# Where the q, k and v loads of a block are issued, in a sliding-window attention kernel with a highway layer

## The chip, the cores and the metric

The kernel runs on one core of a Trainium2 chip. The metric is the device time of one execution in microseconds. The core has TensorE (matmul, written PE in the profile, with PEld for its weight loads), VectorE (DVE), ScalarE (ACT), GpSimd (POOL) and SyncE (SP), each with an instruction queue of its own that is worked off in order; they are coupled by semaphores. Transfers run on the core's 16 DMA engines. Here GpSimd issues almost all loads, and SyncE issues the stores.

## What is computed

Attention over 4 batches, 8 heads, 768 positions of width 64, with a causal window of 128 positions and 4 sink positions at the start of each sequence; its output, 3072 tokens of 512 numbers, goes through a highway layer:

```
scores = scale * np.matmul(q, k.transpose(0, 1, 3, 2))
keep = (pos[None, :] < n_sink) | ((rel >= 0) & (rel < window))     # rel = pos[:, None] - pos[None, :]
a = exp(where(keep, scores, -1e9) - max);  a = a / (a.sum() + 1e-9)
x = np.matmul(a, v)                                                # as 3072 x 512
H = np.maximum(x @ w_h, 0.0)
T = 1.0 / (1.0 + np.exp(-(x @ w_t + b_t)))
out = T * H + (1.0 - T) * x
```

## The kernel before

The 3072 tokens are 24 blocks of 128. Each block goes through the same steps, and the steps of several blocks overlap. The order is written out by hand: `ORDER` (lines 676 to 704) is a list of entries such as `S:12`, step and block, and a loop (line 709) calls the function that `STEP` (line 652) has for each. Inside the schedule each engine works off its own instructions in exactly this order; semaphores are set where one engine needs another's result. So an entry that is moved past another matters only if both put instructions on the same engine.

The steps, with n the block:

- `S` (`pe_S`, TensorE): transposes of the q and k of a later block (`pe_T`, L323; which one, `hosted` says: from block 8 on, q and k of block n+2; before that q of n+1 and k of n+2), then the scores (L376, and L389 for the edges), all into one PSUM tile from block 9 on.
- `xx` (ScalarE, L403; in early blocks two halves `x0_`, `x1_`, L398): exp of the scores. `tt` (ScalarE, L335; in early blocks `tq`, `tk`, L328): the copy of the transposes to SBUF. `mm` (VectorE, L409; early `m0_`, `m1_`): the mask, in place.
- `A` (`do_A`): `pe_A` on TensorE, the product with v: the edge part `pe_AB` (L434, with v of blocks n-1 and n+1), the block's own v (L453) and the sinks (L459). From block 9 on it begins with `pe_bias` (L442) for the highway gate of block n-1. After `pe_A`, `do_A` issues loads on GpSimd.
- `xh` (VectorE, L467 and L472): reciprocal and normalisation. `X` (TensorE, L486) transposes it, `xT` (ScalarE) or `xTV` (VectorE) copies it out (L491).
- `Mt` and `Mh` (TensorE, L502 and L514): the two 512x512 products of the highway layer. `u` (ScalarE, L507): tanh of the gate. `d` (VectorE, L520): max(H, 0) - x. `U` (VectorE, L526): u + 1. `e` (L531): its product with d. `o` (L536): twice x plus that; then the store, on SyncE's queue.
- `sk`, `es`: scores and exp of the sinks. When k of a new sequence's first block has been transposed, GpSimd fills the sink keys (`fill_ks`, L347, two copies) and the sink values (`sink_v`, L186).

Loads: `load_q`, `load_k`, `load_v` (L112, L119, L126) read fp32 from HBM and write fp16 to SBUF; a k or v block that spans two sequences takes two transfers. The blocks up to 8 have buffers of their own and are loaded at the start, in a fixed order (lines 194 to 238). From block 9 on q and k have three buffers each (`late_pool`), so the load of block m waits until block m-3 has been transposed, and v has five (`v_ring`). q of block 9 is not transposed in an `S`, but in a step of its own, `Tq:9`, which stands between `S:7` and `S:8`. A load waits at the head of GpSimd's queue, and whatever GpSimd has to do after it waits behind it.

Before the change all three loads of a step are issued in `do_A`, in the order v of block n+4, q of block n+6, k of block n+6.

At the start VectorE prepares masks and constants. Two of them concern the change: `ones_row` and `ones2`, with which TensorE adds the gate's bias (`bt16`, two copies of the bias on rows 0 and 64). `ones_row` has row 0 at one and takes one 128-row product; `ones2` is a copy of it with row 64 at one besides, for two products of 64 rows.

Of the kernel before, what the change touches and what calls it, by code (L numbers as in the profile page):

```python
# [8 lines left out]
FP16 = mybir.dt.float16  # L9
# [11 lines left out]
def kernel(  # L21
# [18 lines left out]
    nc = tc.nc  # L40
    P = 128

    B, H, S, D = q.shape
# [10 lines left out]
    NB = NT // P  # L54
# [4 lines left out]
    AHEAD = 8  # L59

    const = ctx.enter_context(tc.tile_pool(name="const", bufs=1))
# [25 lines left out]

    ctx.callback(close_s)
    HP = P // 2
    B0 = 9  # L90
    M0 = 9
    FIRST = 9
    NV = FIRST + 5
# [6 lines left out]
    def vi(n):  # L100
        return n if n < FIRST else FIRST + (n - FIRST) % (NV - FIRST)

    def chunk_parts(n):
        b, c = divmod(n, NSC)
        if c:
            return [(slice(0, P), b, c * P - HP)]
        return ([(slice(0, HP), b - 1, S - HP)] if b else []) + ([(slice(HP, P), b, 0)] if b < B else [])

    def load_q(n):
        b, c = divmod(n, NSC)  # L110
        qsd = (sd_pool if n < FIRST else late_pool).tile([P, H, D], FP16, tag="qsd", name="qsd")
        nc.gpsimd.dma_start(out=qsd, in_=q[b, :, c * P:(c + 1) * P, :].transpose([1, 0, 2]))  # L112
        q_sd[n] = qsd

    def load_k(n):
        ksd = (sd_pool if n < FIRST else late_pool).tile([P, H, D], FP16, tag="ksd", name="ksd")
        for rows, b, s0 in chunk_parts(n):
            nr = rows.stop - rows.start
            nc.gpsimd.dma_start(out=ksd[rows], in_=k[b, :, s0:s0 + nr, :].transpose([1, 0, 2]))  # L119
        k_sd[n] = ksd  # L120
# [20 lines left out]
    bt32 = const.tile([P, DM], FP32, tag="bt32")  # L141
    bt16 = const.tile([P, DM], FP16, tag="bt16")
    ones_row = const.tile([P, P], FP16, tag="ones_row")
    ones2 = const.tile([P, P], FP16, tag="ones2")
    kf_first = const.tile([P, H, D], FP32, tag="kf0", name="kf0")
    ident32 = const.tile([P, P], FP32, tag="ident32")
    ident2 = const.tile([P, P], FP16, tag="ident2")
    ks_bd = [const.tile([P, KW], FP16, tag=f"ks{i}", name=f"ks{i}") for i in range(2)]
    vs_bd = [const.tile([P, H, 65], FP16, tag=f"vs{i}", name=f"vs{i}") for i in range(2)]
# [43 lines left out]
    with tc.manual_schedule(engines={ENG.Pool, ENG.SP}):  # L193
# [7 lines left out]
        for b in range(B):  # L201
            nc.sync.dma_start(out=vs_dn[b], in_=v[b, :, 0:NSINK, :])
        nc.gpsimd.affine_select(
            out=ident, in_=ident, compare_op=ALU.is_equal, fill=0.0,
# [57 lines left out]
    def bias_rows(_):  # L262
        nc.vector.memset(bt16, 0.0)
        nc.vector.memset(ones_row, 0.0)
        nc.vector.memset(ones_row[0:1, :], 1.0)
        nc.vector.tensor_copy(out=ones2, in_=ones_row)
        nc.vector.memset(ones2[HP:HP + 1, :], 1.0)

    def bias_half(_):
        for r in (0, HP):  # L270
# [13 lines left out]
    def m_tile():  # L284
        return m_bank[int(next(m_next))]
# [7 lines left out]
    av_t, xh_of, xT_of, t_of, u_of, h_of, dd_of, ee_of, sk_of = {}, {}, {}, {}, {}, {}, {}, {}, {}  # L293
# [127 lines left out]
    def av_tile(n):  # L421
        if n not in av_of:
            av_of[n] = av_ps.tile([P, 2, 4, P], FP32, tag="av", name="av")
            av_t[n] = av_of[n]
        return av_of[n]

    def pe_AB(n):
        av = av_tile(n)
        nxt = v_ring[vi(n + 1)]
        prv = v_ring[vi(n - 1 if n % NSC else n)]  # L430
        lo, hi = slice(0, HP), slice(HP, P)
        for j in range(H):
            for src, part, vt, h in ((lo, hi, nxt, j), (hi, lo, prv, (j + 4) % H)):
                nc.tensor.matmul(  # L434
                    av[part, h // 4, h % 4, 0:_AVN], lhsT=e_at(n, h)[src, P:EW],
                    rhs=vt[src, 65 * h:65 * h + _AVN], start=(h % 4 == 0), stop=False,
                    skip_group_check=True)

    def pe_bias(n):
        t_of[n] = m_tile()  # L440
        for rows in (slice(0, HP), slice(HP, P)):
            nc.tensor.matmul(t_of[n][rows, :], lhsT=ones2[rows, rows], rhs=bt16[rows, :],  # L442
                             start=True, stop=False, skip_group_check=True)

    def pe_A(n):
        if n >= B0:
            pe_bias(n - 1)
        pe_AB(n)
        av = av_of[n]
        vt = v_ring[vi(n)]  # L450
        b, c = divmod(n, NSC)
        for h in range(H):
            nc.tensor.matmul(  # L453
                av[:, h // 4, h % 4, 0:_AVN], lhsT=e_at(n, h)[:, 0:P],
                rhs=vt[:, 65 * h:65 * h + _AVN], start=False,
                stop=False, skip_group_check=True)
        if c:
            for g in range(2):
                nc.tensor.matmul(  # L459
                    av[:, g, :, 0:65], lhsT=es_of[n],  # L460
                    rhs=vs_bd[b % 2][:, 4 * g:4 * g + 4, :], start=False, stop=True,
                    skip_group_check=True)
        av_of[n] = av.rearrange("p g h e -> p (g h) e")
# [167 lines left out]
    def new_T(m, g):  # L631
        if g and m and m % NSC == 0 and m < NB:
            fill_ks(m // NSC, nc.gpsimd)
            sink_v(m // NSC, nc.gpsimd)

    def do_A(n):
        pe_A(n)
        if FIRST <= n + 4 <= NB:
            load_v(n + 4)
        if AHEAD <= n + 6 < NB:  # L640
            load_q(n + 6)
        if FIRST <= n + 6 <= NB:
            load_k(n + 6)

    def norm(n):
        dve_rec(n)
# [2 lines left out]
    def spare(t):  # L649
# [5 lines left out]
        "tqV": lambda n: copy_T(n, 0, nc.vector.tensor_copy),  # L655
        "tkV": lambda n: copy_T(n, 1, nc.vector.tensor_copy),
        "xx": act_SS, "tt": both_T, "mm": dve_masks,
        "S": pe_S, "x0_": lambda n: act_S(n, 0), "x1_": lambda n: act_S(n, 1),
        "m0_": lambda n: dve_mask(n, 0), "m1_": lambda n: dve_mask(n, 1),
        "sk": pe_sink, "es": act_sink, "A": do_A, "xh": norm,  # L660
        "X": pe_X, "xT": act_X, "xTV": lambda n: act_X(n, nc.vector.tensor_copy),
        "Mh": pe_Mh, "Mt": pe_Mt, "u": act_u, "U": dve_U, "d": dve_d, "e": dve_e, "o": dve_o,
        "mz0_": first_mask, "mz1_": second_mask, "id": identities, "ma": clear_ks,
        "na": clear_vs, "mc": bias_rows, "fa": lambda _: fill_ks(0, nc.vector), "fb": bias_half,
        "fc": sink_ones, "fd": lambda _: sink_v(0, nc.vector), "cv": convert_v,
# [9 lines left out]
    }  # L675
    ORDER = """
    mz0_:0 ma:0 na:0 Tq:0 na:1 Tk:0 tq:0 mz1_:0 tk:0 ma:1 wA:0 wA:0 Tk:1 mc:0 cv:0 tk:1 fa:0
    wA:0 wA:0 wA:0 S:0 cv:1 x0_:0 fb:0 x1_:0 wA:0 wA:0 wA:0 wA:0 Tq:3 m0_:0 fc:0 tq:3 wA:0 Tk:2
    tk:2 m1_:0 fd:0 wA:0 wA:0 wA:0 wA:0 Tq:1 A:0 tq:1 S:1 xh:0 sk:1 x0_:1 x1_:1 Tq:2 m0_:1 X:0
    sk:3 xTV:0 es:1 Tk:3 m1_:1 tq:2 tk:3 wA:1 A:1 es:3 S:2 xh:1 x0_:2 x1_:2 Tk:4 m0_:2 sk:2  # L680
    tkV:4 X:1 es:2 m1_:2 S:3 xT:1 A:2 x0_:3 Mh:1 x1_:3 xh:2 tq:4 d:1 X:2 tk:5 Mh:0 xTV:2 m0_:3
    Mh:2 d:0 m1_:3 S:4 d:2 Mt:0 x0_:4 x1_:4 m0_:4 A:3 u:0 m1_:4 Mt:1 tq:5 xh:3 tk:6 U:0 sk:4 u:1
    e:0 S:5 es:4 o:0 X:3 x0_:5 U:1 sk:5 xTV:3 e:1 A:4 x1_:5 m0_:5 o:1 tq:6 Mt:2 xh:4 tk:7 es:5
    u:2 m1_:5 X:4 S:6 xT:4 U:2 e:2 A:5 x0_:6 o:2 Mh:3 x1_:6 xh:5 tq:7 Mh:4 m0_:6 tk:8 m1_:6 X:5
    d:3 S:7 xT:5 d:4 A:6 x0_:7 Mh:5 xh:6 x1_:7 Mt:3 d:5 tq:8 tk:9 m0_:7 X:6 u:3 m1_:7 Mt:5 xT:6
    U:3 e:3 sk:7 o:3 u:5 Tq:9 es:7 U:5 Mt:4 tq:9 e:5 o:5 S:8 u:4 U:4 A:7 x0_:8 e:4 o:4 Mt:6
# [2 lines left out]
    mm:10 u:8 X:9 d:8 S:11 xT:9 U:8 A:10 e:8 xx:11 o:8 sk:11 xh:10 Mt:9 es:11 tt:11 mm:11 Mh:9  # L689
    u:9 X:10 d:9 S:12 xT:10 U:9 A:11 e:9 xx:12 o:9 Mt:10 xh:11 tt:12 Mh:10 mm:12 u:10 X:11 d:10  # L690
    S:13 xT:11 U:10 A:12 e:10 xx:13 o:10 sk:13 xh:12 Mt:11 es:13 tt:13 mm:13 Mh:11 u:11 X:12
    d:11 S:14 xT:12 U:11 A:13 e:11 xx:14 o:11 Mh:12 xh:13 tt:14 Mt:12 mm:14 X:13 d:12 u:12 S:15
    xT:13 U:12 e:12 xx:15 A:14 o:12 sk:15 xh:14 Mt:13 tt:15 mm:15 es:15 X:14 S:16 u:13 xTV:14
    U:13 A:15 xx:16 Mh:14 xh:15 tt:16 Mt:14 d:14 mm:16 Mh:13 u:14 U:14 sk:17 d:13 X:15 es:17
    S:17 xT:15 e:13 e:14 A:16 xx:17 o:13 o:14 Mt:15 xh:16 tt:17 Mh:15 mm:17 u:15 X:16 S:18 d:15
    xT:16 U:15 A:17 xx:18 e:15 o:15 Mh:16 xh:17 tt:18 Mt:16 mm:18 X:17 u:16 S:19 xTV:17 d:16
    A:18 xx:19 U:16 e:16 sk:19 xh:18 Mt:17 es:19 mm:19 tt:19 Mh:17 o:16 u:17 X:18 S:20 d:17
    xT:18 U:17 A:19 xx:20 e:17 o:17 Mh:18 xh:19 tt:20 Mt:18 mm:20 X:19 u:18 S:21 xTV:19 d:18
    A:20 xx:21 U:18 e:18 sk:21 o:18 Mt:19 es:21 xh:20 tt:21 Mh:19 mm:21 u:19 X:20 S:22 d:19
    xT:20 U:19 A:21 xx:22 e:19 o:19 Mh:20 xh:21 tk:24 Mt:20 mm:22 X:21 u:20 S:23 xTV:21 d:20  # L700
    A:22 xx:23 U:20 e:20 sk:23 xh:22 Mt:21 es:23 mm:23 X:22 u:21 Mh:21 xT:22 o:20 A:23 d:21 U:21
# [45 lines left out]
```

## Time and profile before

| what | value |
|---|---|
| median of 3 runs (lowest, highest) | 120.45 us (120.37, 120.69) |
| the profiled execution's own time | 134.59 us |
| its span, first to last instruction | 132.5 us |
| mean granted TensorE clock in it | 0.76 |
| GpSimd, q loads: issues, mean time of one | 23, 908 ns |
| GpSimd, k loads | 26, 856 ns |
| GpSimd, v loads | 26, 853 ns |
| q loads, median from issue to landing | 5.7 us |
| GpSimd waiting for edge matmuls before a v load | 14.0 us, 7 times |
| GpSimd waiting for transposes before a q load | 11.9 us, 2 times |

The profile is one execution, and it took 14 us longer than the runs did. Busy times of an engine are sums of its instructions' durations. [...] A row of the timeline reads: start in us from the span's start, duration in us, engine, line, operation, what it writes and reads, and in brackets how long the engine was idle before it and what ended that.

### The profile page before, as it was taken

The numbers are of one execution on the slowest core, as the hardware profiler recorded it, in microseconds if no ns is written. First come the engines' busy times: TensorE is split into PE (matmuls) and PEld (weight loads), VectorE is DVE, ScalarE is ACT, GpSimd is POOL, SyncE is SP. The second block draws the span as 40 slices with busy tenths as digits, with TensorE's granted clock in tenths as the row PEclk, the third lists the DMA queues.
The fourth block names the chain that finished last, engine by engine and source line by source line (L and its number), as shares of the span: only waits on it lengthen the run. The fifth ranks groups of instructions, "written<-read, shape, count | busy, mean of one in ns | idle before, by whom it ended". The sixth has DMA issues, their size and how long they took to land.

```text
span 132.5 us, 4975 instructions
## 1 busy us (share of the span) xinstructions
PE 122.8 (93%) x2119; PEld 69.7 (53%) x2119; DVE 106.5 (80%) x254; ACT 88.0 (66%) x123; POOL 72.2 (55%) x97
## 2 busy tenths in 40 slices
PE   5998879997999999999999999999999999999940
PEld 2444556444555464754666556647655664565520
DVE  6889745959897769968978797689979978977980
ACT  3356679196696668848977888768769868673120
POOL 6999878589940069926749466596591400000000
PEclk9977777777777777777777777777777777777775
DMA  3999999999999039999599999999999392202122
GB/s 90 217 158 147 161 181 195 155 138 123 185 194 153 2 90 190 190 196 137 56 178 158 153 161 140 171 97 96 180 187 131 103 127 84 79 5 79 54 105 79
DMA packets 79848, 17.64 MB, mean 133 GB/s; under 512 B 75602, under 2 KB 76882, under 8 KB 79828
## 3 DMA queue, kind: packets, MB, share of 16 engines
q0 software_dynamic: 71888, 9.97, 121.7%
q1 hardware_dynamic: 6884, 7.12, 17.7%
q10 hardware_dynamic: 1056, 0.26, 1.2%
q8 instruction: 16, 0.26, 0.8%
q14 instruction: 4, 0.03, 0.1%
HBM read 21.01 MB, written 6.29 MB: 206 GB/s over the span
## 4 chain that ended last, share of the span: by engine, by line
PE 81%; DVE 12%; ACT 2%; issue 2%; DVEq 0%
PE m L514 20%; PE m L502 19%; PE av L453 7%; PE av L434 6%; PE sps L323 5%; PE sps L376 4%; PE av L459 4%; PE sps L389 4%; PE m L358 4%; PE av L486 4%; PE m L499 2%; ACT e L398 1%; DVE u L526 1%; PE m L442 1%; DVE v L178 1%
## 5 line engine op out<-in xcount | busy, mean ns | idle before, releaser
L126 POOL DMA_DIRECT2D v<-in_v_dram x26 | 22.1, 853 | 18.4 <-PE av L434 14.0
L502 PE MATMUL m<-wt_sb,xT 128*128 128x512 f16 x92 | 30.4, 463 | 0.0
L514 PE MATMUL m<-wh_sb,xT 128*128 128x512 f16 x92 | 29.5, 458 | 0.0
L112 POOL DMA_DIRECT2D qsd<-in_q_dram x23 | 20.8, 908 | 11.9 <-PE sps L323 11.9
L403 ACT ACTIVATE e<-sps,ebias 128x1536 f16<-128x1536 f32 x15 | 23.1, 1541 | 4.4 <-PE sps L389 4.3
L409 DVE TENSOR_TENSOR e<-e,mask 128x768 f16<-128x768 f16 (+1 forms) x33 | 23.9, 732 | 2.5 <-ACT e L398 2.5
L507 ACT ACTIVATE u<-m 128x512 f16<-128x512 f32 x23 | 13.8, 598 | 13.7 <-PE m L502 13.7
L119 POOL DMA_DIRECT2D ksd<-in_k_dram x26 | 22.1, 856 | 0.5 <-DMA ksd<-in_k_dram 0.3
L398 ACT ACTIVATE e<-sps,ebias 128x768 f16<-128x768 f32 x18 | 15.2, 897 | 6.7 <-PE sps L389 6.5
L520 DVE SCALAR_TENSOR_TENSOR dd<-m,xh 128x512 f16<-128x512 f32 x23 | 15.8, 688 | 4.6 <-PE m L514 4.4
L472 DVE TENSOR_TENSOR xh<-av,rec 128x512 f16<-128x512 f32 x24 | 16.6, 691 | 0.8
L514 PEld LDWEIGHTS <-xT 128*128 128x128 f16 x92 | 10.0, 112 | 12.1 <-issue 10.8
L536 DVE SCALAR_TENSOR_TENSOR otok<-xh,ee 128x512 f32<-128x512 f16 x23 | 15.8, 689 | 0.6
L502 PEld LDWEIGHTS <-xT 128*128 128x128 f16 x92 | 9.9, 110 | 11.4 <-issue 10.8
L335 ACT COPY tt<-sps 128x1024 f16<-128x1024 f16 x13 | 13.0, 997 | 0.0
L434 PE MATMUL av<-v,e 64*64 64x66 f16 x384 | 11.2, 196 | 1.3 <-DVE xT L491 1.1
L491 ACT COPY xT<-av 128x512 f16<-128x512 f16 x15 | 8.7, 581 | 4.9 <-PE av L486 4.9
L526 DVE TENSOR_SCALAR u<-u 128x512 f16<-128x512 f16 x23 | 9.2, 400 | 2.9 <-ACT u L507 2.8
L434 PEld LDWEIGHTS <-e 64*64 64x64 f16 x384 | 9.5, 109 | 2.9 <-issue 2.3
L328 ACT COPY t<-sps 128x512 f16<-128x512 f16 x19 | 10.3, 589 | 1.1 <-PE sps L323 1.1
L453 PE MATMUL av<-v,e 128*128 128x66 f16 x192 | 10.7, 198 | 0.0
L486 PEld LDWEIGHTS <-xh 64*128 64x128 f16 x192 | 4.2, 95 | 11.6 <-DVE e L409 7.9
(94 smaller groups left out, 183.3 us busy)
## 6 DMA issues: line engine op xcount, KB each, us to landing
out_dram<-otok SPq DMA_DIRECT2D x23, 256.0 KB, 3.2
qsd<-in_q_dram POOLq DMA_DIRECT2D x23, 128.0 KB, 5.7
ksd<-in_k_dram POOLq DMA_DIRECT2D x19, 128.0 KB, 5.7
v<-in_v_dram POOLq DMA_DIRECT2D x19, 128.0 KB, 5.4
wh_sb<-in_moe_w_h_dram POOLq DMA_DIRECT2D x1, 512.0 KB, 7.5
wt_sb<-in_moe_w_t_dram POOLq DMA_DIRECT2D x1, 512.0 KB, 8.9
ksd<-in_k_dram POOLq DMA_DIRECT2D x7, 64.0 KB, 5.2
v<-in_v_dram POOLq DMA_DIRECT2D x7, 64.0 KB, 5.5
```

Of the source, the lines that this page charges most:

```text
L112: nc.gpsimd.dma_start(out=qsd, in_=q[b, :, c * P:(c + 1) * P, :].transpose([1, 0, 2]))
L119: nc.gpsimd.dma_start(out=ksd[rows], in_=k[b, :, s0:s0 + nr, :].transpose([1, 0, 2]))
L126: nc.gpsimd.dma_start(out=vt[rows, :, 0:D], in_=v[b, :, s0:s0 + nr, :].transpose([1, 0, 2]))
L398: nc.scalar.activation(out=e_tile(n)[:, g].rearrange("p a b c -> p a (b c)"), in_=s_tile(n, g)[:, :, 0:2 * EW], func=AF.Exp, bias=ebias, s ...
L403: nc.scalar.activation(out=e_tile(n).rearrange("p g a b c -> p (g a) (b c)"), in_=s_of[n][:, :, 0:2 * EW], func=AF.Exp, bias=ebias, scale= ...
L409: nc.vector.tensor_tensor(out=ev, in0=ev, in1=m.unsqueeze(1).to_broadcast([P, k, EW]), op=ALU.mult)
L434: nc.tensor.matmul(av[part, h // 4, h % 4, 0:_AVN], lhsT=e_at(n, h)[src, P:EW], rhs=vt[src, 65 * h:65 * h + _AVN], start=(h % 4 == 0), sto ...
L453: nc.tensor.matmul(av[:, h // 4, h % 4, 0:_AVN], lhsT=e_at(n, h)[:, 0:P], rhs=vt[:, 65 * h:65 * h + _AVN], start=False, stop=False, skip_g ...
L472: nc.vector.tensor_tensor(out=xh.rearrange("p (h d) -> p h d", d=D), in0=av_of.pop(n)[:, :, 0:D], in1=rec_of.pop(n).unsqueeze(2).to_broadc ...
L502: nc.tensor.matmul(t_of[n], lhsT=xT[:, kc, :], rhs=wt_sb[:, kc, :], start=False, stop=(kc == NOC - 1), skip_group_check=True)
L514: nc.tensor.matmul(hps, lhsT=xT[:, kc, :], rhs=wh_sb[:, kc, :], start=(kc == 0), stop=(kc == NOC - 1))
L520: nc.vector.scalar_tensor_tensor(out=dd, in0=h_of.pop(n), scalar=0.0, in1=xh_of[n], op0=ALU.max, op1=ALU.subtract)
```

## The change

Three things are changed. First, the loads: q of block n+5 is issued behind `S:n`, v of block n+4 behind `A:n` as before, and k behind `d`, where the blocks are counted through in order (each `d`, in the order in which they stand, takes the next k, the first one block 7; those below 9 are loaded at the start and left out). Ahead of a k load GpSimd copies one element of that `d`'s result into a tile `turn`. Second, `ones2` goes: `ones_row` now has row 0 at one in its first 64 columns and row 64 at one in its last 64, and serves both kinds of product. Third, the bias products move from `pe_bias` into `pe_AB`, at the same place; the table `T_BESIDE` names the same blocks as `B0` did, and with `LATE` at 99 the second branch is not taken. In `ORDER` some neighbours are exchanged; of these only one exchange concerns two steps on the same engine, `cv:1` and `fb:0` on VectorE at the start: the bias is now scaled (L271) before the v of block 1 is converted (L178).

```
-        nc.vector.memset(ones_row[0:1, :], 1.0)
-        nc.vector.tensor_copy(out=ones2, in_=ones_row)
-        nc.vector.memset(ones2[HP:HP + 1, :], 1.0)
+        nc.vector.memset(ones_row[0:1, 0:HP], 1.0)
+        nc.vector.memset(ones_row[HP:HP + 1, HP:P], 1.0)
...
+        m = T_BESIDE.get(n)
+        if m is not None:
+            t_of[m] = m_tile()
+            if n < LATE:
+                for part in (lo, hi):
+                    nc.tensor.matmul(
+                        t_of[m][part, :], lhsT=ones_row[part, part], rhs=bt16[part, :],
+                        start=True, stop=False, skip_group_check=True)
...
+    def do_S(n):
+        pe_S(n)
+        if AHEAD <= n + 5 < NB:
+            load_q(n + 5)
+
+    k_next = iter(range(AHEAD - 1, NB + 1))
+
+    def do_d(n):
+        dve_d(n)
+        m = next(k_next, None)
+        if m is not None and m >= FIRST:
+            nc.gpsimd.tensor_copy(out=turn, in_=dd_of[n][0:1, 0:1])
+            load_k(m)
+
     def do_A(n):
         pe_A(n)
         if FIRST <= n + 4 <= NB:
             load_v(n + 4)
-        if AHEAD <= n + 6 < NB:
-            load_q(n + 6)
-        if FIRST <= n + 6 <= NB:
-            load_k(n + 6)
...
-    wA:0 wA:0 wA:0 S:0 cv:1 x0_:0 fb:0 x1_:0
+    wA:0 wA:0 wA:0 S:0 fb:0 x0_:0 cv:1 x1_:0
```

More of the change, by code (lines that the diff above doesn't have):

```diff
@@ L89 @@
     HP = P // 2
-    B0 = 9
+    T_BESIDE = {9: 8, 10: 9, 11: 10, 12: 11, 13: 12, 14: 13, 15: 14, 16: 15, 17: 16, 18: 17, 19: 18, 20: 19, 21: 20, 22: 21, 23: 22}
+    LATE = 99
     M0 = 9
@@ L143 @@
     ones_row = const.tile([P, P], FP16, tag="ones_row")
-    ones2 = const.tile([P, P], FP16, tag="ones2")
     kf_first = const.tile([P, H, D], FP32, tag="kf0", name="kf0")
     ident32 = const.tile([P, P], FP32, tag="ident32")
+    turn = const.tile([1, 1], FP16, tag="turn")
     ident2 = const.tile([P, P], FP16, tag="ident2")
@@ L437, in pe_AB @@
                     skip_group_check=True)
[L439 to L443, printed above, removed]
+            if m is not None and n >= LATE and j % 2 == 0:
+                cols = slice(D * j, D * j + 2 * D)
+                for part in (lo, hi):
+                    nc.tensor.matmul(
+                        t_of[m][part, cols], lhsT=ones_row[part, part], rhs=bt16[part, cols],
+                        start=(j == 0), stop=False, skip_group_check=True)
     def pe_A(n):
-        if n >= B0:
-            pe_bias(n - 1)
         pe_AB(n)
@@ L657 @@
         "xx": act_SS, "tt": both_T, "mm": dve_masks,
-        "S": pe_S, "x0_": lambda n: act_S(n, 0), "x1_": lambda n: act_S(n, 1),
+        "S": do_S, "x0_": lambda n: act_S(n, 0), "x1_": lambda n: act_S(n, 1),
         "m0_": lambda n: dve_mask(n, 0), "m1_": lambda n: dve_mask(n, 1),
@@ L661 @@
         "X": pe_X, "xT": act_X, "xTV": lambda n: act_X(n, nc.vector.tensor_copy),
-        "Mh": pe_Mh, "Mt": pe_Mt, "u": act_u, "U": dve_U, "d": dve_d, "e": dve_e, "o": dve_o,
+        "Mh": pe_Mh, "Mt": pe_Mt, "u": act_u, "U": dve_U, "d": do_d, "e": dve_e, "o": dve_o,
         "mz0_": first_mask, "mz1_": second_mask, "id": identities, "ma": clear_ks,
@@ L677 @@
     mz0_:0 ma:0 na:0 Tq:0 na:1 Tk:0 tq:0 mz1_:0 tk:0 ma:1 wA:0 wA:0 Tk:1 mc:0 cv:0 tk:1 fa:0
-    wA:0 wA:0 wA:0 S:0 cv:1 x0_:0 fb:0 x1_:0 wA:0 wA:0 wA:0 wA:0 Tq:3 m0_:0 fc:0 tq:3 wA:0 Tk:2
+    wA:0 wA:0 wA:0 S:0 fb:0 x0_:0 cv:1 x1_:0 wA:0 wA:0 wA:0 wA:0 Tq:3 m0_:0 fc:0 tq:3 wA:0 Tk:2
     tk:2 m1_:0 fd:0 wA:0 wA:0 wA:0 wA:0 Tq:1 A:0 tq:1 S:1 xh:0 sk:1 x0_:1 x1_:1 Tq:2 m0_:1 X:0
@@ L682 @@
     Mh:2 d:0 m1_:3 S:4 d:2 Mt:0 x0_:4 x1_:4 m0_:4 A:3 u:0 m1_:4 Mt:1 tq:5 xh:3 tk:6 U:0 sk:4 u:1
-    e:0 S:5 es:4 o:0 X:3 x0_:5 U:1 sk:5 xTV:3 e:1 A:4 x1_:5 m0_:5 o:1 tq:6 Mt:2 xh:4 tk:7 es:5
+    e:0 S:5 es:4 o:0 X:3 x0_:5 U:1 sk:5 xTV:3 e:1 A:4 x1_:5 m0_:5 o:1 tq:6 Mt:2 tk:7 xh:4 es:5
     u:2 m1_:5 X:4 S:6 xT:4 U:2 e:2 A:5 x0_:6 o:2 Mh:3 x1_:6 xh:5 tq:7 Mh:4 m0_:6 tk:8 m1_:6 X:5
@@ L691 @@
     S:13 xT:11 U:10 A:12 e:10 xx:13 o:10 sk:13 xh:12 Mt:11 es:13 tt:13 mm:13 Mh:11 u:11 X:12
-    d:11 S:14 xT:12 U:11 A:13 e:11 xx:14 o:11 Mh:12 xh:13 tt:14 Mt:12 mm:14 X:13 d:12 u:12 S:15
+    d:11 S:14 xT:12 U:11 A:13 e:11 xx:14 o:11 Mh:12 xh:13 tt:14 Mt:12 mm:14 X:13 u:12 d:12 S:15
     xT:13 U:12 e:12 xx:15 A:14 o:12 sk:15 xh:14 Mt:13 tt:15 mm:15 es:15 X:14 S:16 u:13 xTV:14
@@ L696 @@
     xT:16 U:15 A:17 xx:18 e:15 o:15 Mh:16 xh:17 tt:18 Mt:16 mm:18 X:17 u:16 S:19 xTV:17 d:16
[L697 to L701, printed above, removed]
+    A:18 xx:19 U:16 e:16 sk:19 xh:18 Mt:17 es:19 mm:19 tt:19 Mh:17 o:16 u:17 X:18 S:20 xT:18
+    d:17 U:17 A:19 xx:20 e:17 o:17 Mh:18 xh:19 tt:20 Mt:18 mm:20 X:19 u:18 S:21 xTV:19 d:18 A:20
+    xx:21 U:18 e:18 sk:21 o:18 Mt:19 es:21 xh:20 tt:21 Mh:19 mm:21 u:19 X:20 S:22 d:19 xT:20
+    U:19 A:21 xx:22 e:19 o:19 Mh:20 xh:21 tk:24 Mt:20 mm:22 X:21 u:20 S:23 xTV:21 d:20 A:22
+    xx:23 U:20 e:20 sk:23 Mt:21 xh:22 es:23 mm:23 X:22 u:21 Mh:21 xT:22 o:20 A:23 d:21 U:21
     Mt:22 xh:23 e:21 X:23 u:22 Mh:22 xTV:23 o:21 Ta:23 d:22 Ha:23 ua:23 U:22 e:22 Tb:23 da:23
```

## The prediction

> **What bounds the kernel now.** I read the page from the top, then the waits, then timelines of VectorE, GpSimd and TensorE for the stretches that the change touches.
>
> ```profile
> span 132.5 us, 4975 instructions
> ...
> PE 122.8 (93%) x2119; PEld 69.7 (53%) x2119; DVE 106.5 (80%) x254; ACT 88.0 (66%) x123; POOL 72.2 (55%) x97
> ...
> PEclk9977777777777777777777777777777777777775
> ...
> PE 81%; DVE 12%; ACT 2%; issue 2%; DVEq 0%
> ```
>
> The profiled execution took 134.59 us: its span of 132.5 and 2.1 around it. In it TensorE ran at a granted clock of 0.75 after the first 7 us and was busy without a gap from 40 to 125 us, so it bounds that execution, and the chain says so. The median of the runs shown is 120.45 us, 14.1 less, a span of about 118.4. Nothing in the code explains that but the clock: 122.8 us at 0.76 is 93 us at full clock, while VectorE's 106.5 us doesn't scale and is 90% of 118.4. So in the timed runs I take VectorE as the bound from about 40 us on, with latency chains before that, and I price each step in microseconds of VectorE or of a chain. At the profile's clock the same steps cost less, since TensorE covers them (55 to 99 us: PE 44.00 of 44, DVE 36.67).
>
> VectorE's `u + 1` (L526, "U") shows what the loads do to it. It runs 23 times, at best in 282 ns, 400 ns in the mean: 9.2 us where 6.5 would do. (First line: the group in the page; then timelines of VectorE and GpSimd: start, duration, instruction.)
>
> ```profile
> L526 DVE TENSOR_SCALAR u<-u 128x512 f16<-128x512 f16 x23 | 9.2, 400 | 2.9 <-ACT u L507 2.8
> ...
> 99.52 0.59 DVE L526 TENSOR_SCALAR u<-u 128x512 f16<-128x512 f16 x1
> ...
> 98.39 0.91 POOL L126 DMA_DIRECT2D v<-in_v_dram  x1
> 99.27 0.72 POOL L119 DMA_DIRECT2D ksd<-in_k_dram  x1
> ```
>
> U wanted the engine at 99.52, GpSimd had been issuing since 98.39, and U ended 0.1 us after that issue did. The seven lengthened ones are at 29.99 (+0.41), 31.78 (+0.84, beside GpSimd's sink product L186), 36.50 (+0.48), 49.35 (+0.20), 62.98 (+0.26, L186 again), 71.84 (+0.13) and 99.52 (+0.30): 2.6 us, of which 1.7 before 37 us. At 58.77 U started 12 ns ahead of an issue and took 293 ns[...].
>
> The third view is the stretch in which the rings are first reused.
>
> ```profile
> 47.45 0.89 POOL L112 DMA_DIRECT2D qsd<-in_q_dram  x1 [9.43 <-PE sps L323]
> 48.33 1.39 POOL L119 DMA_DIRECT2D ksd<-in_k_dram  x2
> 49.68 0.92 POOL L126 DMA_DIRECT2D v<-in_v_dram  x1
> ...
> 46.86 0.29 PE L323 MATMUL sps<-ident,qsd 64*128 64x64 f16 x8
> ...
> 53.32 0.32 PE L323 MATMUL sps<-ident,ksd 64*128 64x64 f16 x8
> ```
>
> GpSimd waited 9.43 us: q of block 12 needs the slot of q 9, which is transposed by step Tq:9 at 46.86 to 47.15. The k of block 11 had been issued at 36.24 and landed at 41.9; it is first read at 53.32, in S:9.
>
> [...] U and casts stretch beside an issue, while the mask (L409), `e` and `o` keep their times (e 409 to 426 ns, o 679 to 693). [...] here a load takes 3.6 us at best and 5.7 in the median from issue to landing[...].
>
> **The change part by part.** TensorE's and ScalarE's sequences keep their order and count; the bias matmuls stay where they were, with `ones_row` for `ones2`. SP's queue of stores isn't touched.
>
> *Start.* VectorE loses the copy L266 (0.29) and one memset's width; from L265 at 7.72 to the cast L178 at 8.49 it takes 0.77 us now, two small memsets of 0.17 take 0.4: the cast comes 0.37 earlier. VectorE has no idle time from 5 to 13.5 us and the chain runs through its casts, L271 and the first masks into A:0. What is late next is q of block 1, landed at 12.31, transposed at 12.36; A:0 waited at 12.58 for the second mask (12.35 to 12.89), so at most 0.4 us comes through. The swapped cast and bias scaling meet other GpSimd issues: L271 took 0.75 instead of 0.41 beside one, and if the cast meets it now, nothing is won. Between -0.4 and 0; I take -0.3.
>
> *Issues of a block.* Before: v, q, k in a row behind A(n), 0.89 each, starting 0.35 us after the edge matmuls L434. After: k behind d(n), behind a 1x1 copy ("turn") that waits for d; q behind the transposes of S; v behind A. GpSimd runs in order, so q and v stand behind k and thus behind d as well. In a usual block (8 to 12, 16) VectorE runs d, U back to back (71.23, 71.84)[...], and k, q, v (2.7 us) lie under e, o, reciprocal, xh and mask (0.46+0.61+0.84+0.86 = 2.8 us). Before, the row began about as U ended, so these blocks are equal; the lengthenings at 71.84 and 99.52 go: -0.43. The three early ones stay, as their issues wait for landings or stand at the same place; so do those beside L186.
>
> Turn runs 15 times. No such copy is in the trace; two ks copies of 64x16 take 0.55, so 0.1 to 0.28 each. On GpSimd (55% busy) it is covered; below nothing it can't be. If e and o keep it from reading SBUF, it starts 1.1 us later: a rival below.
>
> *New meetings.* From 48.4 us GpSimd has 13 issues in a row (k11, v10, k12 in two, q13, v11, k13, q14, v12 in two, k14, q15, v13), about 12 us, where k11 and v10 were long done before; U:7 at 58.77 then meets k14 or q15, +0.6 at most, I take 0.3. Where q follows S without a d ahead of it, at S:16 and S:18, q is issued 0.3 us after its transposes (84.46, 94.43), at 84.76 and 94.73, with U at 84.81 and 94.70: races, 0.85 at most each, I take 0.3 and 0.2. U:12 waits for ScalarE 0.55 us after its d, and k 19 can start in that gap: 0.15. Together +0.95, less the 0.43: +0.5 on VectorE, of which 0.4 on the path at 80 to 90% load.
>
> *k of block 11.* Its turn (d:4) is ready at about 41 us, but q12 stands ahead of it and still waits for Tq:9. So q12 goes at 47.45, turn at 48.35, k11 at 48.45 instead of 36.24. Second loads after an idle queue took 4.8 to 5.0 (59.64 to 64.43, 33.65 to 38.61): it lands at 53.3. At the profile's clock S:9 wants it at 53.32: no wait. In the timed runs S:9 comes when xh:7 is done: u:4 0.35 after a shorter Mt:4, then U, e, o, reciprocal, xh, which puts its k transposes at 52.2: TensorE waits 1.05 us. Behind it stand S:9's scores, A:8 and the next Mt and Mh; xx:9 on ScalarE waits for the scores, xh:8 for A:8. VectorE has both masks of block 8, d:6, U, e, o in the meantime, 3.0 us, which covers nearly all. Between 0 and 1.05; I take 0.4.
>
> *k of block 20.* Its place in the new count is d:14, one block ahead of its use in S:18, behind ks fill and sink product (tt:16 ended 87.69, so fill 87.7 to 89.5). Issue 89.6, landing after 3.9 to 4.9 us at 93.5 to 94.5; use at 94.38. Between 0 and 0.5; I take 0.1. The other k have two blocks.
>
> *Sum:* -0.3 + 0.4 + 0.4 + 0.1 = +0.6 us on the timed runs: 121.0 us (121.05 rounded down, since every term is soft). At the profile's clock only the start would show: about 134.3.
>
> **The rivals.**
> Slower by 0.3 to 1.9 us, the sum above: 121.0. For it: k11's place behind a wait that is known to end at 47.15. Against: VectorE's cover.
> Slower, turn shut out: e and o each read two SBUF inputs; if turn must wait for both, k, q, v start 1.1 us later, reach past the next U and cost 0.3 to 0.6 in ten blocks: +3 to +6, some of it covered, 123.5. Against it: L186 on GpSimd ran beside the mask without either changing much.
> No change: start and meetings cancel, k11 wholly covered: 120.4. For it: TensorE, ScalarE and most issues keep their places.
> Faster, on the other side: one mechanism, v against U. Where the xT copy is on VectorE between mask and U, U starts 1.03 us after the mask (0.42 + 0.61), v's issue 0.88 after it (edge matmuls 0.5, then 0.35): U loses 0.7. At xTV:17 the new turn puts v behind d, so U wins. In the timed runs, with edge matmuls at full clock, the same may hold in blocks without xTV, where U's lead is only 0.27 us. It decides from two such blocks on; with three, and the start: -0.3 - 2.0 + 0.8 = -1.5, 118.95; with one or two 119.6. I take 119.5.
>
> **How the numbers follow.** A difference of 0.3% (0.36 us) is about what a measurement of this kernel can tell. Slower by the sum 0.41, by turn 0.07: 0.48. Within 0.3%: 0.17. Faster: 0.35. Predicted is the likeliest, 121.0; its own range is 120.8 to 122.4. The range over all cases goes from 119.4 (most of the faster case) to 122.4 (k11 and all races at their upper ends).
>
> **What would show it.** Right: k of block 11 issued at about 48.4, TensorE idle at S:9 with its landing as releaser; an unbroken row of issues to 60 us; U at 0.28 in blocks 8 to 12, longer at U:7, U:13, U:15; the first mask ahead of 11.7. Wrong: no wait for a k landing at all, the lengthened U gone after 50 us, or GpSimd's turn waiting for more than d. If the sum of U's times falls by over 1 us, the forecast falls with it.

## The result and the profile after

The changed kernel takes 127.69 us in the median of 4 runs (125.26 to 128.81). The kernel before, run beside it, takes 120.41 (119.60 to 120.69, 4 runs). The ratio is 1.0474, with a 95% interval from 1.0341 to 1.0608. The comparison leaves out executions more than 1.5% above a kernel's fastest; here those are the ones that were hit hardest, so the medians differ by more (7.3 us) than the ratio says (5.7 us).

The profiled execution after took 128.67 us, its span 126.4. First the page: the span, the busy times, the slices with the granted clock, and the share of each engine in the chain that ended last.

```profile
span 126.4 us, 5014 instructions
...
PE 109.8 (87%) x2119; PEld 66.3 (52%) x2119; DVE 104.1 (82%) x253; ACT 87.6 (69%) x123; POOL 78.0 (62%) x113
...
PEclk9999999999999999689999999999958999999999
...
PE 43%; DMA 15%; DVE 13%; POOL 12%; issue 9%; ACT 4%; DVEq 0%; POOLq 0%; ACTq 0%
```

Against the page before: this execution has the full clock nearly throughout, so it isn't slower because of what held the first profile's clock to 0.76. The clock digits dip in two places, near 53 us and near 94 us. And transfers, absent from the chain of the page before, are 15% of it, 9% of them loads of k. The waits say which (in all, times, longest, in us):

```profile
POOL turn L653 <- DVE dd L526: 12.4, 7, 3.9
...
DVE rec L473 <- PE av L465: 7.7, 6, 3.4
PEld L323 <- DMA ksd<-in_k_dram: 5.8, 3, 3.2
...
PE sps L323 <- DMA ksd<-in_k_dram: 5.2, 3, 3.0
```

GpSimd's wait for `d` in the first row is how k's place is defined, and no loss by itself. TensorE waits 5.2 us for k, in three places: 3.03, 1.73 and 0.4. VectorE waits 7.7 us for the product with v that comes behind, 3.4 of them at once. The first place is S:9. TensorE's timeline there:

```profile
43.08 0.29 PE L323 MATMUL sps<-ident,qsd 64*128 64x64 f16 x8
...
48.35 0.28 PE L323 MATMUL sps<-ident,qsd 64*128 64x64 f16 x8
48.47 0.28 PE L376 MATMUL sps<-t,t 64*128 64x128 f16 x4
51.77 0.39 PE L323 MATMUL sps<-ident,ksd 64*128 64x64 f16 x8 [3.03 <-DMA ksd<-in_k_dram]
```

The first row is Tq:9, the other three are S:9: q transposed, half of the scores, then 3.03 us of nothing until k of block 11 is there. GpSimd's timeline has its issue, and the chain of waits its landing:

```profile
43.67 0.87 POOL L113 DMA_DIRECT2D qsd<-in_q_dram  x1 [3.79 <-DVE otok L542]
44.54 0.41 POOL L653 COPY turn<-dd 1x1 f16<-1x1 f16 x1
44.89 0.87 POOL L120 DMA_DIRECT2D ksd<-in_k_dram  x1
```

```profile
44.89 6.83 DMA ksd<-in_k_dram
51.72 0.05 issue
51.77 0.39 PE sps L323 x6
```

GpSimd stood idle for 3.79 us with q of block 12 at the head of its queue. (The profile names VectorE's `otok` as what ended this; the transposes of Tq:9 ended at 43.37, 0.3 us before the issue, as in the profile before, where they were named. A step that waits for several things is put down to the last semaphore event.) Then came turn and k of block 11, whose issue takes GpSimd 0.87 us; from the issue's start to the landing it took 6.83 us. The second place is S:18, on TensorE:

```profile
88.94 0.28 PE L376 MATMUL sps<-tt 64*128 64x128 f16 x4
90.95 0.29 PE L323 MATMUL sps<-ident,ksd 64*128 64x64 f16 x8 [1.73 <-DMA ksd<-in_k_dram]
...
92.35 1.92 PE L520 MATMUL m<-wh_sb,xT 128*128 128x512 f16 x4
94.06 1.80 PE L508 MATMUL m<-wt_sb,xT 128*128 128x512 f16 x4
```

Here k of block 20 is late by 1.73 us. The rows that follow show a second loss: four products of L520 take 1.92 us, where four of the same took 1.03 at 87.74. With each of the two waits comes a stretch of 3.41 us in which the clock is at half (51.25 to 54.66 and 92.21 to 95.62 in the clock's record). By windows, whose clock column stands ahead of the DMA share:

```profile
50.00:55.00 5.00, 3.23 (x64) 2.72 (x65) 1.53 (x4) 1.59 (x2) 3.91 (x6) 0.66 2.10 198
...
90.00:95.00 5.00, 4.05 (x63) 2.15 (x64) 3.32 (x7) 2.44 (x2) 3.35 (x5) 0.72 1.98 200
```

For a comparison at the same clock the kernel before was run again under a new label. Its profiled execution took 120.42 us (span 118.6, clock 0.991). How far `after` is behind it can be read off the starts of `d` on VectorE, which come in the same order in both:

| the same d in | before, again | after | behind by |
|---|---|---|---|
| last one ahead of the wait in S:9 | 48.12 | 48.74 | 0.62 |
| first one behind it | 51.82 | 55.92 | 4.10 |
| next | 55.93 | 61.04 | 5.11 |
| last one ahead of the wait in S:18 | 85.21 | 89.34 | 4.13 |
| first one behind it | 89.24 | 96.47 | 7.23 |
| last d of the kernel | 113.82 | 121.64 | 7.82 |

So 3.5 us come with the wait in S:9, 1.0 in the block behind it, in which the half clock goes on, 3.1 with the wait in S:18 and its half clock, and 0.6 each before the first and after the second. Between the two, 1.0 us is won back. The steady blocks in between run at VectorE's pace: `d` starts at 65.49, 69.18, 72.87 and 76.57 after, 3.69 to 3.70 apart. In the kernel before the same steps are 3.70, 3.73 and 4.51; in the last of them TensorE stood idle for 1.08 us, and the profile shows nothing that it waited for. That is most of what is won back.

### The profile page after: what moved, and what is told of

Its sections match the earlier page's. It is cut to its first block, busy times and chain, and to the rows that moved or that the text cites. A ratio compares the mean times of both kernels' runs of the same rounds, so it can differ in the third digit from the quotient of the medians.

```text
span 126.4 us, 5014 instructions
## 1 busy us (share of the span) xinstructions
PE 109.8 (87%) x2119; PEld 66.3 (52%) x2119; DVE 104.1 (82%) x253; ACT 87.6 (69%) x123; POOL 78.0 (62%) x113
## 4 chain that ended last, share of the span: by engine, by line
PE 43%; DMA 15%; DVE 13%; POOL 12%; issue 9%; ACT 4%; DVEq 0%; POOLq 0%; ACTq 0%
PE m L520 9%; DMA ksd<-in_k_dram 9%; PE m L508 7%; DMA qsd<-in_q_dram 6%; PE av L459 5%; PE av L442 4%; POOL qsd L113 4%; DVE xh L478 3%; PE sps L323 3%; ACT e L398 3%; PE sps L389 3%; POOL ksd L120 3%; PE av L465 2%; PE sps L376 2%; POOL v L127 2%
## 5 line engine op out<-in xcount | busy, mean ns | idle before, releaser
L508 PE MATMUL m<-wt_sb,xT 128*128 128x512 f16 x92 | 24.4, 389 | 0.0
L520 PE MATMUL m<-wh_sb,xT 128*128 128x512 f16 x92 | 24.2, 390 | 0.0
L520 PEld LDWEIGHTS <-xT 128*128 128x128 f16 x92 | 8.8, 99 | 9.2 <-issue 1.4
L508 PEld LDWEIGHTS <-xT 128*128 128x128 f16 x92 | 8.9, 100 | 8.7 <-issue 1.1
L653 POOL COPY turn<-dd 1x1 f16<-1x1 f16 x16 | 5.4, 337 | 12.4 <-DVE dd L526 12.4
L473 DVE RECIPROCAL rec<-av 128x8 f32<-128x8 f32 x24 | 4.9, 203 | 9.6 <-PE av L465 7.7
L323 PE MATMUL sps<-ident,ksd 64*128 64x64 f16 x184 | 6.8, 192 | 5.6 <-DMA ksd<-in_k_dram 5.2
```

The costliest lines, as they stand in the source:

```text
L508: nc.tensor.matmul(t_of[n], lhsT=xT[:, kc, :], rhs=wt_sb[:, kc, :], start=False, stop=(kc == NOC - 1), skip_group_check=True)
L520: nc.tensor.matmul(hps, lhsT=xT[:, kc, :], rhs=wh_sb[:, kc, :], start=(kc == 0), stop=(kc == NOC - 1))
```

## The experiments

The theory to be tested ("late k"): two loads decide, k of block 11 and k of block 20. Its rivals: the waits are an accident and the cost is in what the new order does in every block, above all `turn`; or the cost is in the edits at the start.

**The kernel before, once more.** No edit; it gives the comparison above, and a profile at the timed clock.

> The kernel before, unchanged, for a profile at the clock of the timed runs. Every theory: ratio 1.00. Theory of the two late k loads: no wait of TensorE for a k landing after 40 us, and the granted clock stays at full from 40 us on. Theory of the meetings with VectorE: its lengthened u+1 amount to 5 us less than in the changed kernel (there 1.6 us in all, so this theory needs other VectorE instructions to be shorter too).

Measured: 120.90 us (119.30 to 123.24, 20 runs) against 120.99, ratio 0.9949 (0.9914 to 0.9984). Two labels of one kernel differ by half a per cent, so a single ratio below that means little here. In its trace nothing waits for k after 40 us:

```profile
36.68 0.91 POOL L119 DMA_DIRECT2D ksd<-in_k_dram  x1
...
43.20 0.89 POOL L112 DMA_DIRECT2D qsd<-in_q_dram  x1 [4.74 <-PE sps L323]
```

k of block 11 is issued at 36.68, ahead of the wait of 4.74 us, and not behind it. It landed at 42.65 and is first read at 48.11.

**Each k by itself.** First, q of block 12 is issued where its buffer comes free, behind Tq:9, so that k of block 11 no longer stands behind a wait:

```
     def do_S(n):
         pe_S(n)
-        if AHEAD <= n + 5 < NB:
+        if AHEAD <= n + 5 < NB and n != 7:
             load_q(n + 5)
...
+    def do_Tq(n):
+        pe_T(("t", n, 0), 0, q_sd.pop(n))
+        if n == FIRST:
+            load_q(n + 3)
...
```

> The changed kernel with q of block 12 issued right behind the transposes of q 9 that free its buffer, so that k 11 no longer stands behind its wait. Theory of the two late k loads: the wait of 3.2 us in S:9 and the slow stretch behind it go, and 2.5 to 4.5 us of the 5.7 come back, about 122. Theory of turn and meetings: all 16 turns are still there, so at most 0.5 us comes back. Theory of a general crowding of the transfers: the same bytes at nearly the same places, at most 1 us.

Measured: 123.53 us (122.11 to 125.01, 4 runs), ratio 1.0144 (1.0053 to 1.0234). The wait in S:9 is gone. The one in S:18 is there, with the half clock behind it:

```profile
87.70 0.29 PE L323 MATMUL sps<-ident,ksd 64*128 64x64 f16 x8 [1.56 <-DMA ksd<-in_k_dram]
...
89.15 1.92 PE L520 MATMUL m<-wh_sb,xT 128*128 128x512 f16 x4
```

The four times fall in two pairs: 122.11 and 122.17 at a mean clock of 1.0, and 124.89 and 125.01 at 0.971 and 0.986. The half clock goes with up to 2.8 us; in the trace of the execution at 125.01 the step over S:18, from one `d` to the next, takes 6.89 us where it takes 4.03 in the kernel before. That is 2.86 for a wait of 1.56, so that at least 1.3 is the half clock.

Second, the other way round, k of block 20 alone is issued behind S:15 and left out of the count:

```
             load_q(n + 5)
+        if n == 15:
+            load_k(20)
...
-        if m is not None and m >= FIRST:
+        if m is not None and m >= FIRST and m != 20:
```

> The changed kernel with k of block 20 issued behind the scores of block 15, without a turn, instead of behind the second next highway difference. Theory of the two late k loads: the wait of 1.9 us in S:18 goes, and with it the half-clock stretch at 92 to 96 us: 1.5 to 3.5 us come back, about 123.5. Theory of turn and meetings: one turn less, 0.2 us. Theory of crowding: at most 0.5 us.

Measured: 124.22 us (121.87 to 124.33, 4 runs; the comparison gives no ratio). The wait in S:18 is gone, the one in S:9 stays at 2.65 us, with half clock from 50.36 to 53.77. Again one run at clock 0.999 took 121.87, and three at 0.974 to 0.985 took 124.2 to 124.3. So each load costs by itself, and neither removes the other's wait.

**Both k in time.** Both edits together, all else as in the changed kernel, `turn` with all its other places included:

> Both edits together. Theory of the two late k loads: 5 to 7 us come back, 119.5 to 121, within 1% of the kernel before, and the chain shows no k landing. Theory of turn and meetings or of crowding: still at least 3% slower than before, about 124 to 125.

Measured: 121.82 us (120.11 to 122.98, 4 runs), 1.0149 (1.0053 to 1.0245). Four runs were too few beside this spread, so it was run again later:

> The kernel with both late k moved forward and the turns kept, again, to tell 1.0149 apart from 1.0028, which the same kernel without turn had. If turn has a price of its own: 1.005 to 1.015; if not: 1.000 to 1.005.

Measured: 121.54 us (119.49 to 127.03, 22 runs), 0.9997 (0.9959 to 1.0035). No difference from before. TensorE in S:9, from the profiled execution of the first (120.11 us):

```profile
47.82 0.28 PE L323 MATMUL sps<-ident,qsd 64*128 64x64 f16 x8
47.94 0.28 PE L376 MATMUL sps<-t,t 64*128 64x128 f16 x4
48.05 0.28 PE L323 MATMUL sps<-ident,ksd 64*128 64x64 f16 x8
```

There is no gap, and the clock record is full:

```profile
PEclk9999999999999999999999999999999999999996
```

The chain of this kernel's first profile has no load of k, and that of its second only one issued at 30 us. The placing of these two loads thus accounts for the whole loss, within what the comparison resolves.

**Without turn.** The copy is taken out of both, of the kernel with both k early and of the changed kernel as it is:

```
         if m is not None and m >= FIRST:
-            nc.gpsimd.tensor_copy(out=turn, in_=dd_of[n][0:1, 0:1])
             load_k(m)
```

> The kernel with both late k moved forward, and without the turn copies: k stays behind d in GpSimd's order but doesn't wait for it. Theory that what is left (121.8 against 121.0) is the price of turn: 0.5 to 1 us comes back, 121.0 or below. Theory that it is the spread of the runs or landings that are only just in time: no change beyond 0.5 us.

Measured: 121.12 us (119.85 to 123.29, 22 runs), 1.0028 (0.9997 to 1.0059). With turn it was 0.9997, without it 1.0028, and the intervals overlap: where k is in time, turn costs nothing that shows.

> The changed kernel without the turn copies; both late k keep their places in GpSimd's order. Theory of the two late k loads: k 11 still stands behind q 12, so the wait in S:9 stays; k 20 no longer waits for a highway difference but still stands behind the sink fill; at most 1.5 us comes back. Theory of turn: 16 turns are 5.4 us of GpSimd and hold back every k, so 3 us or more come back.

Measured: 123.15 us (122.02 to 125.56, 4 runs), 1.0168 (1.0087 to 1.0249). The changed kernel itself was run beside it:

> The changed kernel, unchanged, to have its time beside the next ones on one chip. Theory of the two late k loads: 125 to 128 us again, two waits of TensorE for a k landing, in S:9 and in S:18; runs in which the clock halves twice are 2 to 3 us longer than runs in which it doesn't.

Measured: 125.42 us (124.71 to 128.09, 4 runs), 1.0368 (1.0298 to 1.0438). Its trace has both waits again: 1.70 us in S:9 with the half clock behind it, and 1.44 in S:18, this time at full clock. So leaving turn out gives back 2.3 us by the medians, between what the two theories expected. In the trace without turn GpSimd reaches k of block 20 earlier, and the wait in S:18 is down to 0.56 us:

```profile
82.25 1.03 POOL L187 TENSOR_TENSOR vs<-vd,bm 32x512 f16<-32x512 f32 x1
83.24 1.81 POOL L120 DMA_DIRECT2D ksd<-in_k_dram  x2
```

```profile
87.09 0.29 PE L323 MATMUL sps<-ident,ksd 64*128 64x64 f16 x8 [0.56 <-DMA ksd<-in_k_dram]
```

The k landed at 87.04, 3.80 us after its issue (4.50 in `after_again`). The wait in S:9 stays, at 1.58 us, since what holds k of block 11 back is q's wait for Tq:9; but no half clock follows it here. What turn itself adds is small: 0.35 us ahead of k of block 11 (44.54 to 44.89 in `after`), and 0.3 ahead of k of block 20 (from the start of the sink product to k's issue it is 1.30 us with turn and 0.99 without). So turn's price is not one per block; it adds to the lateness of these two loads. The rest of the 2.3 us isn't turn's own time: against the kernel before, the stretch of S:9 costs 3.5 us in the trace with turn and 1.6 in the one without, that of S:18 1.2 and 0.2. How much of this turn causes, and how much is chance from one execution to the next, isn't shown.

**The same lateness in the kernel before.** Nothing of the change but k of block 11 behind the wait:

```
         if AHEAD <= n + 6 < NB:
             load_q(n + 6)
-        if FIRST <= n + 6 <= NB:
+        if FIRST <= n + 6 <= NB and n != 5:
+            if n == 6:
+                load_k(11)
             load_k(n + 6)
```

> The kernel before, with only k of block 11 moved: issued behind q of block 12, which waits for the buffer of q 9, as the change has it; no turn, no other load moved. Theory of the late k loads: TensorE waits 1.5 to 2.5 us in S:9 for its landing and, where the granted clock halves behind that, loses 1.5 us more: +1.5 to +4 us over the kernel before. Theory of turn and meetings: none is added, so within 0.4 us of the kernel before.

Measured: 122.38 us (121.75 to 124.36, 4 runs), 1.0186 (1.0123 to 1.0248). TensorE and VectorE in its trace:

```profile
50.23 0.29 PE L323 MATMUL sps<-ident,ksd 64*128 64x64 f16 x8 [1.52 <-DMA ksd<-in_k_dram]
```

```profile
51.77 0.21 DVE L467 RECIPROCAL rec<-av 128x8 f32<-128x8 f32 x1 [1.05 <-PE av L459]
```

k was issued at 44.51 and landed at 50.18. The one move costs 1.8 us by the medians. The profiled execution has no half clock behind the wait (the window from 48 to 55 us has it at 1.00). In the kernel before, once more, the same reciprocal starts at 50.11, without any idle time ahead of it: the result it needs (A:8's last product, 49.38 to 49.77) is there only 0.34 us ahead. That is all the cover there is: of a wait of 1.52 it leaves 1.2 us. So it comes out at first: the `d` ahead of the wait is 0.43 us behind the kernel before (48.55 against 48.12), the one behind it 1.66 (53.48 against 51.82). One block on even this cover is used up, since VectorE waits again, 0.27 us for the next transposes of X: that `d` is 2.01 behind (57.94 against 55.93). The wait of 1.52 us has cost 1.6.

**Is it the idle time or the half clock behind it?** In the changed kernel 12 spare products on a constant tile were put on TensorE ahead of S:9's k transposes, so that it is busy while it would wait:

```
         for g in range(2):
+            if g and n == 9:
+                fill_9()
...
+    def fill_9():
+        t = m_bank[int(M_BANKS[m_taken[0]])]
+        for _ in range(12):
+            nc.tensor.matmul(t, lhsT=warm[:, 0:P], rhs=warm, start=True, stop=True)
...
```

> The changed kernel with 12 extra matmuls on a constant tile (2.6 us at full clock, results unused) in TensorE's queue right ahead of the k transposes of S:9, where it waits 3 us for k 11. The landing doesn't move, so the wait's end doesn't either. If the halved clock behind the wait is a cost of its own, caused by the idle time, the clock stays at full there and 1 to 2.5 us come back, about 125.5 to 126.5; if the wait alone costs, nothing comes back, 127 to 128; if the extra matmuls push S:9 out, it is slower.

Measured: 125.30 us (124.10 to 126.83, 4 runs), 1.0413 (1.0341 to 1.0485).

```profile
48.22 2.75 PE L293 MATMUL m<-warm 128*128 128x512 f16 x12
50.90 0.29 PE L331 MATMUL sps<-ident,ksd 64*128 64x64 f16 x8
```

```profile
48.00:55.00 7.00, 7.00 (x114) 3.80 (x107) 4.63 (x9) 3.56 (x6) 5.47 (x8) 1.00 2.05 195
```

```profile
50.90 0.17 PEld L331 LDWEIGHTS <-ksd 64*128 64x128 f16 x8 [0.42 <-DMA ksd<-in_k_dram]
```

The rows are the products, the window and the weight load. TensorE is busy for all of the 7 us and the clock stays at 1.00. The filler holds nothing up, since the weight load behind it still waits 0.42 us for k. `d` is 0.15 us behind the kernel before ahead of this place (48.27), 2.34 behind it (54.16) and 2.69 at the next (58.62): 2.5 us for k's lateness alone. In `after` it was 4.5, with a wait 0.4 us longer. (The medians of the two kernels, on different chips and with waits of different length, don't resolve this.)

The same stretch can be read in every trace. From the `d` ahead of the wait in S:9 to the second one behind it the kernel before takes 7.81 us, and so do the kernels here that have no wait there (7.81 or 7.82). What the others take beyond that:

| trace | wait in S:9 | beyond 7.81 us | clock behind the wait |
|---|---|---|---|
| without three stores (below) | 0.68 | 0.6 | full |
| kernel before, k 11 late | 1.52 | 1.6 | full |
| without turn | 1.58 | 1.6 | full |
| wait filled | 2.6, filled | 2.5 | full |
| changed kernel, again | 1.70 | 3.5 | half |
| k 20 early | 2.65 | 4.1 | half |
| changed kernel | 3.03 | 4.5 | half |

At full clock the waits in S:9 cost their own length within 0.1 us. With the half clock behind them 1.5 to 1.8 us more are lost. At S:18 it is alike: waits of 1.44, 1.59 and 1.74 us at full clock cost 1.2 to 1.4 there (against the step of 4.03 in the kernel before), waits of 1.56 and 1.73 with the half clock 2.9 and 3.1. So both cost time: the idle time about what it lasts, and a stretch at half clock some 1.5 to 1.8 us on top.

**Why does k take so long to land?** The changed kernel without the stores of blocks 3, 4 and 5, whose output rows stay unwritten. These stores, 256 KB each, are moved in the stretch in which q of block 12 and k of block 11 are:

```
-        nc.sync.dma_start(out=out[n * P:(n + 1) * P, :], in_=otok)
+        if n not in (3, 4, 5):
+            nc.sync.dma_start(out=out[n * P:(n + 1) * P, :], in_=otok)
```

> The changed kernel without the stores of blocks 3, 4 and 5, 768 KB that are written from 43.5 to 51 us, while q 12 and k 11 are loaded; those rows of the output are left unwritten. If k 11 takes 6.8 us instead of the 4.8 that was forecast because these stores share the DMA engines, it lands 1 to 2 us earlier after its issue and the wait in S:9 shrinks to 1 to 2 us; if the loads alone make it slow, landing and wait stay as they are.

Measured: 122.53 us (121.70 to 123.27, 4 runs), 1.0146 (1.0072 to 1.0220). The chain of waits has k at

```profile
44.35 4.48 DMA ksd<-in_k_dram
```

and q of block 12 lands 3.49 us after its issue (43.13 to 46.62; 4.71 in `after`). The wait in S:9 is down to 0.68 us; the one in S:18 stays, at 1.59. With all stores k took 6.83 and 5.50 us in the two traces of the changed kernel, and 6.46 with k of block 20 early. So the stores, moved at the same time, cost k of block 11 between 1.0 and 2.4 us in these executions.

**The edits at the start alone.** The kernel before, with `ones_row` for both products and `cv:1` and `fb:0` exchanged, nothing else:

```
-        nc.vector.memset(ones_row[0:1, :], 1.0)
-        nc.vector.tensor_copy(out=ones2, in_=ones_row)
-        nc.vector.memset(ones2[HP:HP + 1, :], 1.0)
+        nc.vector.memset(ones_row[0:1, 0:HP], 1.0)
+        nc.vector.memset(ones_row[HP:HP + 1, HP:P], 1.0)
...
```

> The kernel before with only the edits at the start: one ones_row for both products, and the bias scaled ahead of the conversion of v. As predicted: 0.3 us faster, between 0 and 0.4, the first mask ahead of 11.7 us. Rival: the conversion meets a GpSimd issue and nothing is won.

Measured: 120.27 us (119.76 to 122.97, 17 runs), 1.0023 (0.9988 to 1.0058). No difference. The first mask does start earlier, at 11.02 us against 11.74 in the kernel before, but the first reciprocal starts at 13.76, against 13.80. Nothing of the 7 us lies at the start, and nothing is won there.

None of these versions is faster than the kernel before.

## Why the prediction was right and wrong

*Right: the side, the two places and why k is late there.* The forecast had two loads of k arrive late, those of blocks 11 and 20, with TensorE waiting in S:9 and S:18, and that is what the trace shows and what the kernel with both k early confirms. The guess that the first profile's clock was not that of the timed runs holds: the same kernel, once more, took 120.42 us at a clock of 0.991, and its S:9 wants k of block 11 5.21 us after the end of Tq:9 (48.11 less 42.90), where 5.05 had been worked out (52.2 less 47.15). VectorE's busy time is 103.3 us there, against 106.5 in the first profile, so it hardly follows TensorE's clock. TensorE's is 107.3 against 122.8, where 93 had been worked out.

*Wrong: the size.* +0.6 us was predicted and +7.3 measured; 127.69 lies outside the range. Three things failed in the sum.

The term "k of block 11", 0.4 us between 0 and 1.05. Two of its steps failed. First its landing: "4.8 to 5.0" us had been taken from two loads that followed an idle queue, where k of block 11 itself had taken 5.65 at its old place and the page's median was 5.7 for q. It took 6.83, 6.46, 5.50 and, in the kernel before with k late, 5.67 us. Of this the stores were shown to be 1.0 to 2.4 us; without three of them it took 4.48. They aren't the whole account: one of the two loads that the forecast went by (33.65 to 38.61) had a store beside it too, which landed at 38.51. Stores of SyncE were not in the forecast at all, except for the sentence that their queue isn't touched. Their queue isn't, but three of them, 256 KB each, are issued at 43.52, 44.94 and 47.07 us in `after`, where k of block 11 is issued at 44.89 and lands at 51.72. Second the cover: VectorE has "3.0 us" of work in the meantime, and that was counted as cover. It isn't, since VectorE does that same work while TensorE does its own, wait or no wait. Cover is only the time by which a result is there before it is wanted: 0.34 us here, and one block on even that was lost. With the measured values the term is 1.6 us for the wait of 1.52 (the kernel before with k late), and about 3.0 for the 3.03 us in the profiled execution after, where k took longest (an estimate: the waits at full clock cost their own length).

The term "k of block 20", 0.1 us between 0 and 0.5. Its place one block ahead of its use, behind `fill_ks`, `sink_v` and turn, was read right. So was its landing: 4.74 us after the issue, where 3.9 to 4.9 had been put. But TensorE's side was taken at the profile's low clock, with the use 4.8 us after the issue (94.38 less 89.6). At full clock TensorE would have had it 3.1 us after the issue (90.95 less the wait of 1.73, less 86.16). For S:9 the forecast had converted the times to the timed clock; for S:18 it hadn't. Measured: a wait of 1.73 us, 1.44 in the repeat, which at full clock cost 1.2 us.

A term was missing. No wait was given a price beyond its own length, and TensorE's products behind a wait were taken to run at full speed. Here a stretch of 3.41 us at half clock followed waits of 1.56 to 3.03 us in some executions, and none followed others of 1.44 to 1.74. What tells these apart the traces don't show. The stretches in the clock's record are multiples of 3.413 us: 44.37, 37.55 and 30.72 us at full clock in `after`, 13, 11 and 9 times that, and 122.88 us at 0.75 in the first profile, 36 times. How busy TensorE was in the 3.41 us ahead doesn't settle it. In the following lines of `after` the second figure is the stretch's length, the third TensorE's busy time, and the clock stands ahead of the DMA share:

```profile
47.84:51.25 3.41, 0.90 (x23) 0.35 (x20) 2.89 (x7) 1.30 (x3) 3.41 (x5) 1.00 1.68 176
88.80:92.21 3.41, 1.68 (x76) 1.35 (x75) 2.75 (x5) 1.41 (x3) 3.41 (x5) 1.00 1.70 232
119.51:122.93 3.42, 1.66 (x16) 1.24 (x13) 3.28 (x9) 0.77 (x2) 0.00 (x0) 1.00 0.29 113
122.93:126.34 3.41, 0.00 (x0) 0.00 (x0) 0.46 (x2) 0.00 (x0) 0.00 (x0) 1.00 0.33 118
```

The clock fell behind the first, with 0.90 us of work and the wait in S:9, and behind the second, with 1.68 us and the wait in S:18. Behind the third, with 1.66 us near the kernel's end, it stayed at 1.00 for all of the fourth. So whether a wait of about 1.6 us brings the half clock can't be forecast from these traces. The missing term is 1.5 to 1.8 us for each stretch at half clock. In the profiled execution after, the two places together, waits and half clock, are 4.5 and 3.1 us, where the forecast had 0.4 and 0.1. Over whole runs of the kernel with q of block 12 at its slot the executions at lower clock are 2.8 us longer, more than one such stretch; what makes up the difference stays open, since only one execution of that kernel has a trace.

*Start, -0.3 us.* The first mask came 0.7 us earlier (11.01, against 11.74 in the kernel before at full clock), yet the first reciprocal came no earlier (14.02 against 13.80). The forecast itself named what is late next, q of block 1; it left 0.3 us to be won, and there was none: in `after` q of block 1 landed at 12.91 and is the start of the chain.

*New meetings with VectorE's U, +0.4 us.* U's total is 8.1 us after, 7.4 in the kernel before once more (323 ns each) and 7.9 and 7.6 with both k early: +0.2 to +0.7 where +0.5 had been put, though partly in other blocks. The size was about right, and with both k early it doesn't show in the time. That of a U and an issue the one that starts first keeps its time was the author's estimate, from cases such as U at 99.52 and at 58.77 in the first profile; no run tests it.

```profile
L532 DVE TENSOR_SCALAR u<-u 128x512 f16<-128x512 f16 x23 | 8.1, 353 | 0.9 <-ACT u L513 0.8
```

```profile
L526 DVE TENSOR_SCALAR u<-u 128x512 f16<-128x512 f16 x23 | 7.4, 323 | 1.0 <-ACT u L507 0.8
```

The first line is the group of the changed kernel, the second that of the kernel before, once more.

*The rivals.* Turn shut out for all of `e` and `o`, ten times: it isn't. It runs 16 times, not 15, and takes 337 ns in the mean, 0.18 us at best and 0.72 at worst; where it began beside an `o` it ended within 0.05 us of that `o`'s end, six times (at 50.12 to 50.84, for one, beside an `o` from 50.11 to 50.80). Faster, with v against U: at full clock U was lengthened by only 0.77 us in one place in the kernel before, against the 2.6 us in the first profile, so there was nothing to win. That rival rested on the low clock, as did the use of k in S:18.

## What to carry to other kernels

When a load is moved in a queue that works in order, ask what it now stands behind: its issue is as late as the worst wait ahead of it, and its landing has to be compared with its first use at the clock of the timed runs, with the traffic of that stretch, stores included. An engine's queued work is no cover for another's wait unless its inputs lie ready longer than the wait lasts; read the time between "result there" and "result used", not the busy time. And where TensorE is made to wait one or two microseconds, count the wait once, and 1.5 to 1.8 us more for the executions in which a stretch at half clock follows, as it did here after waits of 1.56 us and more, though not after every one.

## What the runs showed that had not been expected

- TensorE went to half clock for 3.41 us after idle times of 1.56, 1.70, 1.73, 2.65 and 3.03 us, and did not after 1.44, 1.52, 1.58, 1.59 and 1.74 us. So the length alone doesn't decide. Kept busy where it would have waited in S:9 (7.00 of the 7 us from 48 to 55 in the filled kernel), TensorE had its clock at 1.00.
- The kernel before has executions at a lower clock as well: 3 of the 20 of its repeat took over 123 us, at mean clocks of 0.956 to 0.985 where the profiled one had 0.991. None of them has a trace, so where they lose it isn't known.
- A 128 KB load from GpSimd took 3.49 us (q of block 12) and 4.48 us (k of block 11) without three stores of 256 KB beside it, and 4.71 and 6.83 us with them in the first profile after.
- A copy of one element on GpSimd took 0.18 us in 8 of 16 cases, none of them begun beside VectorE's `o`, and 0.41 to 0.72 in the six begun beside one, and the load behind it often began only 0.3 us after its end ("issue" in the timeline: 5 times, 1.5 us in all).
